# A new head for a fused top-k attention and mixture-of-depths kernel: first rows in order of need, PSUM tiles per head, products that nobody reads, smaller fills

## The chip, the cores and the metric

The kernel runs on one core of a Trainium2 chip. Its time is the device time of one execution in microseconds (us). The core has a matrix engine (TensorE, called PE in the profile), VectorE (DVE), ScalarE (ACT), GpSimd (POOL) and a queue engine that issues transfers (SyncE, SP). ACT can issue transfers as well. Each engine works through its own instructions in the order in which they are written; a wait at the front of a queue holds all that is behind it.

## What is computed

The reference is top-k attention over 8 batches and 8 heads, then a gated two-layer network on 128 chosen rows of each batch:

```python
batch, n_heads, seq, head_dim = (8, 8, 576, 64)          # q, k, v, float32
scores = scale * np.matmul(q, k.transpose(0, 1, 3, 2))
kth = np.partition(scores, -32, axis=-1)[..., -32:-31]    # the 32nd largest of each row
scores = np.where(scores >= kth, scores, -1e9)
attn = softmax(scores);  x = (attn @ v), heads side by side   # (8, 576, 512)
s = x @ w_gate                                            # one score per row
top = the 128 rows of each batch with the largest s
out = x;  out[top] += sigmoid(s[top]) * (relu(x[top] @ w1) @ w2)
```

## The kernel before, in words

**Tiling.** A batch's 576 query rows are four tiles of 128 and one of 64 (`t`). Heads go in pairs. A unit is one row tile with one head pair `g` (in the last, half-filled row tile, with four heads), so a batch has 4 x 4 + 2 = 18 units and the kernel 144 (`units`, `per_batch`). The first four units are row tile 0 of batch 0 with head pairs 0 to 3.

**A unit's way.** PE forms the scores of two heads, 128 x 576 each (`multiply`); ACT copies them from PSUM to the SBUF tile `sc` (`keep`). DVE finds, from maxima of parts of the row, a value `bound` near the 32nd largest (`find_bound`, 14 maxima of 82 or 83 columns, then 10 small steps). ACT compares all scores with it and counts (`sides`), POOL multiplies scores and signs into `y` (`what_is_below`), DVE takes the 8 largest of `y` (`find_kth`), and ACT and POOL mark the scores below the 32nd in `less`, one head each (`mask`). PE transposes scores and adds `less` times a very negative matrix (`weigh`), ACT takes the exponential into `pT`, PE multiplies by `v` (`values`), ACT copies the result to `xs`.

**What sets the order.** The main loop `for n in range(-1, N)` is written out by hand, and the wrapper `InOrder` keeps each engine's instructions in that order. In pass n, DVE does the bound of unit n and the 32nd largest of unit n-2; PE transposes unit n-4, multiplies unit n+1, and does the values of unit n-4; ACT does the exponential of n-4, the mask of n-3, the copy of the scores of n+1, then `sides` of n-1.

**Keys and queries.** Rows of k and q lie in HBM with 64 contiguous floats. They are loaded as rows (`Rows.fetch`, two transfers of 128 KB, one for each head of a pair) and transposed by PE (`Rows.turn`), then copied by ACT into `kT` and `qT` (`Rows.keep`). The rows 512 to 575 of all heads come in a tile of their own, `last` (`turn_last`, `keep_last`). For batch 0 this is done pair by pair ahead of the unit that needs it (`turn_pair`, `turn_all_last`), and the rows stand in the space that the weights `w1` will fill later (`homes`). For the next batches the transposes are cut into 18 parts, which the loop does one or two at a time in spare columns of the scores' PSUM tile (`loads_at`, `first_loads`).

**The head before the change.** SP issues the keys of pair 0, the last rows of k, and then the keys and queries of pairs 1 to 3; ACT issues the queries of pair 0 and the last rows of q. PE runs 48 products of a 128 x 128 bf16 matrix into a tile that nobody reads (`warm_up`); its operand `out_of_reach` is made from the identity, which POOL makes first. Then it transposes all of pair 0 and all last rows, DVE copies the keys, ACT the queries. PSUM has one scores tile of four banks (`ps_sc`), two banks for transposes (`ps_tr`), one for the values (`ps_av`), and one for the rest (`ps_misc`). The first unit's scores are copied half by ACT, half by DVE. POOL fills constants: among them both tiles of `v` (128 x 2,080 floats each) with ones, of which only every 65th is needed.

Of the kernel before, what the change touches and what calls it, by code (L numbers as in the profile page):

```python
# [12 lines left out]
FP32 = mybir.dt.float32  # L13
BF16 = mybir.dt.bfloat16
# [9 lines left out]
SMALLER = 2.0**-20  # L24
# [7 lines left out]
J = 4  # L32
# [16 lines left out]
def kernel(  # L49
# [11 lines left out]
    nc = tc.nc  # L61
    P = nc.NUM_PARTITIONS
    B, H, S, D = q.shape
# [24 lines left out]
        tc.tile_pool(name="dram", bufs=2, space=bass.MemoryType.DRAM)  # L88
    )
    PS = bass.MemoryType.PSUM  # L90
    ps_sc = ctx.enter_context(tc.tile_pool(name="ps_sc", bufs=1, space=PS))
    ps_tr = ctx.enter_context(tc.tile_pool(name="ps_tr", bufs=1, space=PS))
    ps_av = ctx.enter_context(tc.tile_pool(name="ps_av", bufs=1, space=PS))
    ps_misc = ctx.enter_context(tc.tile_pool(name="ps_misc", bufs=1, space=PS))


    ident = const.tile([P, P], FP32, name="ident")
    make_identity(nc, ident)

# [54 lines left out]
    vbufs = []  # L154
    for i in range(2):
        vt = const.tile([P, H, J, DE], FP32, name=f"v{i}")
        nc.gpsimd.memset(vt, 1.0)
        vpair = const.tile([P, NHP, 2, DE], FP32, name=f"vpair{i}")
        nc.gpsimd.memset(vpair, 0.0)
        for hh in range(2):  # L160
            nc.gpsimd.memset(vpair[hh * R : (hh + 1) * R, :, hh, D:DE], 1.0)
        vbufs.append((vt, vpair))

    wg = const.tile([P, HD], FP32, name="wg")
    w1 = const.tile([P, NDC, F], FP32, name="w1")
    w2 = const.tile([P, NFC, HD], FP32, name="w2")

# [46 lines left out]
    class Rows:  # L214
# [1 line left out]

        def __init__(self, kb, qb, kT, qT, issue=None, homes=None):
            self.src, self.kT, self.qT, self.homes = (kb, qb), kT, qT, homes  # L220
            self.last = [
                ldpool.tile([R, H, D], FP32, name=f"last{i}", bufs=1) for i in range(2)
            ]
            self.rows = []
            if issue:
                self.fetch(sp)
                self.fetch(issue)
            for w, dma in enumerate((sp, issue or sp)):
                dma.dma_start(
                    out=self.last[w],  # L230
                    in_=self.src[w][:, JP:S, :].rearrange("h p d -> p h d"),
                )
            while len(self.rows) < (2 * NHP if homes else 2):
                self.fetch()

        def fetch(self, dma=sp):
            i = len(self.rows)
# [20 lines left out]
                    ident[0:R, 0:R],  # L258
                )

        def keep_last(self, w, tr, copy=None):
            copy = copy or act.copy
            tr = tr.rearrange("p b (e r) -> p b e r", e=2)

            def of(a):
                return a.rearrange("p (b e) r -> p b e r", e=2)

            if w == 0:
                copy(out=of(self.kT[:, :, 0:R]), in_=tr)
                copy(out=of(self.kT[:, :, S : S + R]), in_=tr)  # L270
            else:
                act.mul(out=of(self.qT[:, :, JP:S]), in_=tr, mul=SMALLER)
# [12 lines left out]
        def keep(self, i, tr, c0=0, c1=J, copy=None):  # L285
            copy = copy or act.copy
            if i % 2 == 0:
                to = self.kT[:, i // 2, R + c0 * P : R + c1 * P]
            else:
                to = self.qT[:, i // 2, c0 * P : c1 * P]  # L290
            to = to.rearrange("p (c i) -> p c i", i=P)
            if i % 2 == 0:
                copy(out=to, in_=tr)
            else:
                act.mul(out=to, in_=tr, mul=SMALLER)
# [12 lines left out]
                        lambda tr, i=i, c=c: self.keep(i, tr, c, c + 2),  # L308
                    )

    def turn_pair(rows, hp, copy=None):
        tr = ps_tr.tile([P, 2, J, P], FP32, name="ptr")
        for w in range(2):
            rows.turn(2 * hp + w, tr[:, w, :, :])
        for w in range(2):
            rows.keep(2 * hp + w, tr[:, w, :, :], copy=copy)

    def turn_all_last(rows, copy=None):
        tr = ps_misc.tile([P, 2, 2, P], FP32, name="tr", tag="misc")
        for w in range(2):  # L320
            rows.turn_last(w, tr[:, w, :, :])
        for w in range(2):
            rows.keep_last(w, tr[:, w, :, :], copy)

    def load_v(vb, vs):
        vt, vpair = vs
# [25 lines left out]
    def room_for_scores():  # L352
        return ps_sc.tile([P, 2, 2, 512], FP32, name="ps")

    def multiply(t, g, kT, qT, ps):

        n = R if t == J else P  # L360
        for u in range(2):
            for i, heads in enumerate(heads_of(t, g)):
                at = u * HALF + (0 if i else R)
                d = slice(i * D, (i + 1) * D)
                for h, r in heads:
                    pe.matmul(
                        ps[r : r + n, i, u, 0:HALF],
                        qT[d, h // 2, t * P : t * P + n],
                        kT[d, h // 2, at : at + HALF],
                    )  # L370

    def keep(ps, first=False):

        sc = scpool.tile([P, 2, S], FP32, name="sc")
        to = sc.rearrange("p i (u s) -> p i u s", u=2)
        if first:
            for i, copy in enumerate((act.copy, dve.tensor_copy)):
                copy(out=to[:, i, :, :], in_=ps[:, i, :, 0:HALF])
        else:
            act.copy(  # L380
                out=to.rearrange("p i u s -> p (i u) s"),
                in_=ps.rearrange("p i u s -> p (i u) s")[:, :, 0:HALF],
            )
        return sc
# [607 lines left out]


    loads_at = [1, 1, 0, *[1] * 11, 2, 2, 0, 1]
    first_loads = [0, 0, 1, *loads_at[3:]]
    assert sum(loads_at) == sum(first_loads) + 1 == 2 + 4 * NHP
    mix_steps = {}
    for b in range(B - 1):
# [16 lines left out]
    homes = [  # L1015
        homes[:, i, :].rearrange("p (j h d) -> p j h d", j=J, h=2) for i in range(2 * NHP)
    ]
    first_rows = Rows(k[0], q[0], *qkv[0][0:2], issue=act, homes=homes)

    def warm_up():  # L1020
        ps = ps_av.tile([P, 512], FP32, name="av")
        for _ in range(48):
            pe.matmul(ps[:, 0:P], out_of_reach, out_of_reach)

    warm_up()
    turn_pair(first_rows, 0, dve.tensor_copy)
    turn_all_last(first_rows, dve.tensor_copy)
    loading = iter(())
    inverting = normalised = None
    of_batch = {}  # L1030
# [2 lines left out]
    def is_unit(n):  # L1033
        return 0 <= n < N
# [59 lines left out]
    for n in range(-1, N):  # L1094
# [4 lines left out]
                loading, Rows(k[b + 1], q[b + 1], *qkv[b + 1][0:2]).parts()  # L1099
            )  # L1100
        if 0 < n + 1 < NHP:
            turn_pair(first_rows, n + 1)
        if n == 1:
            load_v(v[0], qkv[0][2])
        if n == NHP:
# [21 lines left out]
        flush()  # L1127
        if is_unit(n + 1):
            b, t, g = units[n + 1]
            ps = room_for_scores()  # L1130
            kT, qT = qkv[b][0:2]
            b, i = divmod(n, per_batch)
            loads = list(islice(loading, first_loads[i] if b == 0 else loads_at[i]))
            halves = [ps[:, a, :, HALF : HALF + P] for a in range(2)]
            for load, half in zip(loads, halves):
                load[0](half)
            multiply(t, g, kT, qT, ps)
            for load, half in zip(loads, halves):
                load[1](half)
            scs[n + 1] = keep(ps, n == -1)  # L1140
        if is_unit(n - 4):
            b4, t4, g4 = units[n - 4]
            values(t4, g4, pT, last, av, qkv[b4][2])
# [25 lines left out]
            after_kth.pop(0)()  # L1169


        if is_unit(n - 1):
            what_is_below(n - 1)

        if gating is not None:
# [153 lines left out]
    def general(b, row0):  # L1329
        def of(a):  # L1330
            return a[bass.ds(b, 1)].rearrange("o a s d -> (o a) s d")

        kT, qT, vs = room_for_qkv(0)
        rows = Rows(of(k), of(q), kT, qT)
        turn_all_last(rows)
        for hp in range(NHP):
            turn_pair(rows, hp)
        load_v(of(v), vs)
        x = xpool.tile([P, NT, HD], FP32, name="x")
        pg = gates_of[0]  # L1340
        for t in range(NT):
            xs = xpool.tile([P, H, DE], FP32, name="xs")
            for g in range(groups(t)):
                ps = room_for_scores()
                multiply(t, g, kT, qT, ps)
                p = general_weights(keep(ps))
                tr, av = room_to_turn()
                turn(p, tr)
                pT = ptpool.tile([P, 2, J, P], FP32, name="pT")
                last = ptpool.tile([P, P], FP32, name="last")  # L1350
                nc.scalar.copy(out=pT, in_=tr)
                nc.scalar.copy(out=last, in_=turn_last(p, av))
                values(t, g, pT, last, av, vs)
                keep_values(t, g, av, xs)
            rows = R if t == J else P
            den = stats.tile([P, H], FP32, name="den")
            keep_sums(rows, xs, den[0:rows, :])
            divide(rows, xs, x[0:rows, t, :], den[0:rows, :])
            dot_tile(t, x, pg)
        store(out[bass.ds(b, 1)].rearrange("o s n -> (o s) n"), x)  # L1360
        rank = stats.tile([P, NT], FP32, name="rank")
        for _ in mixture(row0, pg, rank, exact=True):
            flush_all()
        flush_all()
# [40 lines left out]
```

## Time and profile before

| | |
|---|---|
| median of three runs | 826.69 us (826.53 to 827.79) |
| the profiled execution: its own time, its span | 828.44 us, 826.1 us |
| busy share of the span: PE, DVE, ACT, POOL | 94%, 95%, 88%, 87% |
| first maximum on DVE starts | 12.15 us |
| DVE idle from then until 41.44 us | 1.50 + 1.21 + 0.28 us |
| DVE busy from 60 to 80 us, from 300 to 400 us | 20.00 of 20, 99.89 of 100 us |

The span is what the profiler sees between the first and the last instruction; the time of the same execution is 2.3 us longer. "Busy" of an engine leaves out waiting and issuing. The TensorE clock (PEclk) is the share of full speed that the chip granted. Nearly all of the kernel's own instructions stand under one line, L45, the wrapper's, so they are told apart by the tiles that they write and read: `cand<-sc` is a maximum in `find_bound`, `sc<-ps` a copy of scores, `ps<-kT,qT` a product of `multiply`, `ptr<-ident,w` a transpose of first rows.

### The profile page before, as it was taken

How to read it: one execution, taken by the hardware profiler on the slowest of the kernel's cores; microseconds unless marked ns; L12 is line 12 of the kernel's file. 1: busy time of each engine (PE TensorE's matmuls, PEld its weight loads, DVE VectorE, ACT ScalarE, POOL GpSimd, SP SyncE). 2: the span in 40 equal slices, each digit the busy share in tenths (PEclk: the TensorE clock that was granted, in tenths of full speed). 3: DMA queues.
4: the chain of work that ended last, by engine and by line, in shares of the span. 5: the costliest groups of instructions: out<-in, count | busy, mean ns of one | idle time of the engine just before them, and what ended most of it. 6: DMA issues, size and time to landing. Idle time of an engine off the chain costs nothing. (4 is left out here: it accounts for less than half of the span.)

```text
span 826.1 us, 28252 instructions
## 1 busy us (share of the span) xinstructions
PE 777.0 (94%) x10143; PEld 596.5 (72%) x10143; DVE 787.2 (95%) x4651; ACT 730.7 (88%) x1557; POOL 715.4 (87%) x722
## 2 busy tenths in 40 slices
PE   6888888888999999999999999999999999999976
PEld 5566666666887778877787777877787777767744
DVE  7899999999999999999999999999999999999960
ACT  4799999999999999999999999999999999879831
POOL 3799999999899999999899999999999998899831
PEclk9699999999999999999999999999999999999999
DMA  7931111521141221521223221512215102101021
GB/s 170 283 86 40 28 66 28 105 53 27 60 92 36 53 40 59 112 47 34 79 47 86 53 40 60 104 23 54 40 59 112 28 15 66 23 12 18 2 71 30
DMA packets 122133, 50.38 MB, mean 61 GB/s; under 512 B 116417, under 2 KB 116417, under 8 KB 120961
## 3 DMA queue, kind: packets, MB, share of 16 engines
q1 hardware_dynamic: 118672, 43.91, 22.0%
q0 software_dynamic: 1728, 4.20, 2.8%
q8 instruction: 82, 1.34, 0.8%
q14 instruction: 67, 0.54, 0.3%
q10 hardware_dynamic: 1584, 0.39, 0.2%
HBM read 36.93 MB, written 11.55 MB: 59 GB/s over the span
## 5 line engine op out<-in xcount | busy, mean ns | idle before, releaser
L45 POOL TENSOR_TENSOR y<-sc,sides 128x576 f32<-128x576 f32 x288 | 365.1, 1289 | 57.0 <-ACT sides L45 54.3
L45 DVE MAX8 cand<-sc 128x8 f32<-128x82 f32 (+1 forms) x2016 | 314.0, 228 | 2.7 <-ACT sc L45 2.7
L45 POOL TENSOR_SCALAR less<-sc,next 128x576 bf16<-128x576 f32 x135 | 232.5, 1722 | 12.9 <-DVE next L45 10.0
L45 PE MATMUL ptr<-out_of_reach,less 128*128 128x128 bf16 x1136 | 205.3, 220 | 19.5 <-POOL less L45 19.4
L45 ACT ACTIVATE sides<-sc,bound 128x576 bf16<-128x576 f32 x288 | 223.0, 787 | 0.0
L45 PE MATMUL ptr<-ident,sc 128*128 128x128 f32 x1136 | 217.0, 282 | 0.0
L45 DVE MAX8 next<-y 128x8 f32<-128x584 f32 x288 | 204.4, 751 | 1.7 <-POOL y L45 1.6
L45 PEld LDWEIGHTS av<-v,pT 128*64 128x64 f32 x4544 | 144.1, 137 | 66.9 <-ACT last L45 63.2
L45 PE MATMUL ps<-kT,qT 64*128 64x288 f32 (+1 forms) x1280 | 182.0, 431 | 5.2 <-ACT qT L45 5.2
L45 PEld LDWEIGHTS ptr<-ident,sc 128*128 128x128 f32 x1136 | 161.3, 142 | 29.1 <-issue 17.4
L45 ACT ACTIVATE pT<-ptr 128x1024 f32<-128x1024 f32 x142 | 145.3, 1023 | 33.2 <-PE ptr L45 32.2
L45 PE MATMUL av<-v,pT 128*64 128x65 f32 x4544 | 163.7, 224 | 9.3 <-ACT last L45 8.5
L45 ACT COPY sc<-ps 128x1152 f32<-128x1152 f32 (+1 forms) x144 | 162.2, 1126 | 3.5 <-PE ps L45 3.5
L45 PEld LDWEIGHTS <-less 128*128 128x128 bf16 x1296 | 136.1, 106 | 39.2 <-POOL less L45 25.2
L45 PEld LDWEIGHTS ps<-kT,qT 64*128 64x128 f32 (+1 forms) x1280 | 100.2, 178 | 41.5 <-issue 21.2
L45 ACT ACTIVATE less<-sc,next 128x576 bf16<-128x576 f32 x143 | 111.2, 777 | 12.7 <-DVE next L45 10.8
L45 DVE MATCH_REPLACE8 cand<-best,cand 128x21 f32<-128x21 f32 (+1 forms) x576 | 99.0, 180 | 0.0
L45 DVE MAX8 best<-cand 128x8 f32<-128x21 f32 (+1 forms) x576 | 90.5, 190 | 0.0
L45 PE MATMUL h_ps<-xeT,w 128*128 128x128 f32 x464 | 65.8, 286 | 0.0
L45 PEld LDWEIGHTS h_ps<-xeT,w 128*128 128x128 f32 x464 | 55.8, 191 | 9.2 <-issue 5.8
L45 PE MATMUL y_ps<-w,hT 128*128 128x512 f32 x112 | 60.6, 636 | 0.0
L45 ACT ACTIVATION_READ_ACCUMULATOR sides<-sc,bound 128x1 f32 x288 | 59.9, 208 | 0.0
(133 smaller groups left out, 866.4 us busy)
## 6 DMA issues: line engine op xcount, KB each, us to landing
v<-in_v_dram SPq DMA_DIRECT2D x64, 128.0 KB, 4.2
out_dram<-x SPq DMA_DIRECT2D x8, 1024.0 KB, 3.9
rows<-in_k_dram SPq DMA_DIRECT2D x56, 128.0 KB, 2.9
rows<-in_q_dram SPq DMA_DIRECT2D x56, 128.0 KB, 3.1
w<-in_moe_w_dram SPq DMA_DIRECT2D x2, 2048.0 KB
gate_row<-row_dram SPq DMA_DIRECT2D x7, 288.0 KB, 4.4
w<-in_k_dram SPq DMA_DIRECT2D x8, 128.0 KB, 3.2
last<-in_k_dram SPq DMA_DIRECT2D x8, 128.0 KB, 4.0
```

What stands on the lines that cost most here:

```text
L45: return lambda *a, **kw: self._tc.keep_in_program_order(fn(*a, **kw))
```

## The change

The change rewrites what happens until the fifth unit:

- **First rows by need, two queues.** `fetch_first` issues the keys of head 0 on SP and of head 1 on ACT, then on SP the one column of pair 0's queries that row tile 0 needs (64 KB), on ACT the last keys of heads 0 and 1 (32 KB), then the other query columns and last keys on both. The last rows of q come at the end of SP's list.
- **Only what the next unit needs is transposed.** `FirstPairs.first` turns the keys of pair 0, one query column and the last keys of two heads: six transposes instead of sixteen. `turn` does the same for a later pair. The other query columns follow in two blocks, at n = 0 and n = 3, the last rows of q at n = 3.
- **PSUM tiles per head.** The first four units use two tiles of two banks, `one` and `two`, one for each head; ACT copies each head's scores on its own (128 x 576), also the half of unit 0 that DVE copied. The pool is closed after unit 3, and the four banks become `ps_sc`.
- **Unread products in TensorE's gaps.** `stay_busy` runs 30 products at the start, from a part of `wg` that DVE sets to zero, and 10, 10, 20, 30 and 20 after the multiplications of units 0 to 4.
- **`sides` of unit n-1 before the scores of unit n+1** on ACT, in the passes n = 1 and 2.
- **Short fills.** POOL sets only the 32 columns of ones in each `v` tile.
- The 18 parts of batch 1 start one pass later (`first_loads`).

```diff
+    wg = const.tile([P, HD], FP32, name="wg")
+    nothing = wg[:, 0 : P // 2].bitcast(BF16)
+    nc.vector.memset(nothing, 0.0)
...
-        nc.gpsimd.memset(vt, 1.0)
+        nc.gpsimd.memset(vt[:, :, :, D:DE], 1.0)
...
+        def fetch_first(self):
+            k_rows, q_rows = self.homes[0:2]
...
+            sp.dma_start(out=k_rows[:, :, 0, :], in_=of(0, 0, 0, J))
+            act.dma_start(out=k_rows[:, :, 1, :], in_=of(0, 1, 0, J))
+            sp.dma_start(
+                out=q_rows[:, 0, :, :],
+                in_=self.src[1][0:2, 0:JP, :].rearrange("h (p j) d -> p j h d", j=J)[
+                    :, 0, :, :
+                ],
+            )
+            self.fetch_last(0, act, 0, 2)
+            sp.dma_start(out=q_rows[:, 1:J, 0, :], in_=of(1, 0, 1, J))
+            act.dma_start(out=q_rows[:, 1:J, 1, :], in_=of(1, 1, 1, J))
+            self.fetch_last(0, act, 2, H)
+            while len(self.rows) < 2 * NHP:
+                self.fetch()
+            self.fetch_last(1)
...
+        def first(self):
...
+            rows.turn(0, k01, 0, half)
+            rows.turn(0, k23, half, J)
+            rows.turn(1, q0.unsqueeze(1), 0, 1)
+            self.turn_last_keys(range(1), last)
+            rows.keep(0, k01, 0, half, copy=dve.tensor_copy)
+            rows.keep(0, k23, half, J)
+            dve.tensor_scalar_mul(rows.qT[:, 0, 0:P], q0, SMALLER)
+            self.keep_last_keys(range(1), last)
+
+        def turn(self, hp):
+            rows = self.rows
+            keys = bank(ps_av, "av").rearrange("p (c i) -> p c i", i=P)
+            some = bank(ps_misc, "some", tag="misc")
+            rest = range(1, NHP) if hp == 1 else range(0)
+            last = some[:, P : P + len(rest) * R]
+            rows.turn(2 * hp, keys)
+            self.turn_last_keys(rest, last)
+            rows.turn(2 * hp + 1, some[:, 0:P].unsqueeze(1), 0, 1)
+            rows.keep(2 * hp, keys)
+            if rest:
+                self.keep_last_keys(rest, last)
+            rows.keep(2 * hp + 1, some[:, 0:P].unsqueeze(1), 0, 1)
...
-    first_loads = [0, 0, 1, *loads_at[3:]]
+    first_loads = [0, 0, 0, *[1] * 11, 2, 2, 1, 1]
...
-    def warm_up():
-        ps = ps_av.tile([P, 512], FP32, name="av")
-        for _ in range(48):
-            pe.matmul(ps[:, 0:P], out_of_reach, out_of_reach)
-
-    warm_up()
-    turn_pair(first_rows, 0, dve.tensor_copy)
-    turn_all_last(first_rows, dve.tensor_copy)
+    def stay_busy(times, what=out_of_reach):
+        ps = bank(ps_av, "av")
+        for _ in range(times):
+            pe.matmul(ps[:, 0:P], what, what)
+
+    stay_busy(30, nothing)
+    first_pairs.first()
...
         if 0 < n + 1 < NHP:
-            turn_pair(first_rows, n + 1)
+            first_pairs.turn(n + 1)
+        if n == 0:
+            for hp in range(2):
+                first_pairs.turn_queries(hp)
+            for hp in range(2):
+                first_pairs.keep_queries(hp)
+        if n == NHP - 1:
+            for hp in range(2, NHP):
+                first_pairs.turn_queries(hp)
+            for hp in range(2, NHP):
+                first_pairs.keep_queries(hp)
+            first_pairs.last_queries()
+            first_steps.close()
+            ps_sc = ctx.enter_context(tc.tile_pool(name="ps_sc", bufs=1, space=PS))
...
+            if n + 1 < NHP:
+                ps = room_for_first_scores()
+                multiply(t, g, kT, qT, ps)
+                if is_unit(n - 1):
+                    what_is_below(n - 1)
+                stay_busy((10, 10, 20, 30)[n + 1])
+            else:
...
+                if n == NHP - 1:
+                    stay_busy(20)
+            scs[n + 1] = keep(ps)
...
-        if is_unit(n - 1):
+        if is_unit(n - 1) and n + 1 >= NHP:
             what_is_below(n - 1)
```

## The prediction

> **What bounds the kernel now.** I read the page's busy rows first, then the stretches, then the timeline of each engine in the first 45 us.
>
> ```profile
> PE   6888888888999999999999999999999999999976
> DVE  7899999999999999999999999999999999999960
> PEclk9699999999999999999999999999999999999999
> ```
>
> Each digit is a fortieth of the span, 20.7 us. DVE is full except in the first two slices and at the end, so it bounds the kernel: what DVE gains in the first two slices reaches the end, if nobody else becomes the bound. In the second slice the TensorE clock stands at 0.6. The stretches say the same with numbers (columns: busy us of PE, weight loads, DVE, ACT, POOL; clock; DMA):
>
> ```profile
> 20.00:30.00 10.00, 6.68 (x29) 4.28 (x29) 8.47 (x54) 6.97 (x15) 6.22 (x7) 0.55 0.81 209
> 40.00:50.00 10.00, 9.51 (x144) 7.20 (x138) 9.91 (x61) 10.00 (x21) 9.34 (x10) 1.00 0.67 147
> 300.00:400.00 100.00, 98.12 (x1316) 76.01 (x1313) 99.89 (x599) 95.40 (x205) 92.28 (x91) 1.00 0.28 60
> ```
>
> From 300 to 400 us DVE rests 0.11 us, and ACT, the next non-PE engine, has 4.6% to spare. Now DVE's timeline (start, length, what; in brackets the idle time before and who ended it):
>
> ```profile
> 2.63 4.09 DVE L143 CAST steps<-steps_i 128x16 f32<-128x16 int32 x1
> 8.14 0.69 DVE L45 COPY kT<-ptr 128x512 f32<-128x512 f32 x1 [1.41 <-PE ptr L45]
> 11.48 0.76 DVE L45 COPY sc<-ps 128x576 f32<-128x576 f32 x1 [1.94 <-ACT sc L45]
> 12.15 2.13 DVE L45 MAX8 cand<-sc 128x8 f32<-128x82 f32 x14
> 25.39 2.14 DVE L45 MAX8 cand<-sc 128x8 f32<-128x82 f32 x14 [1.50 <-ACT sc L45]
> 36.30 2.14 DVE L45 MAX8 cand<-sc 128x8 f32<-128x82 f32 x14 [1.21 <-ACT sc L45]
> 40.09 1.44 DVE L45 MAX8 next<-y 128x8 f32<-128x584 f32 x2 [0.28 <-POOL y L45]
> ```
>
> DVE starts its real work at 12.15 and then loses 1.50 + 1.21 + 0.28 = 2.99 us until 41.44; after that it hardly waits. Two things to win: an earlier start, and those 2.99 us. The timelines of PE, ACT and POOL name the causes:
>
> ```profile
> 1.69 5.30 PE L45 MATMUL av<-out_of_reach 128*128 128x128 bf16 x48 [1.69 <-DVE out_of_reach L126]
> 6.79 1.31 PE L45 MATMUL ptr<-ident,w 128*128 128x128 f32 x8
> 16.40 1.24 PE L45 MATMUL ps<-kT,qT 64*128 64x288 f32 x8 [1.18 <-ACT qT L45]
> 21.36 2.29 PE L45 MATMUL ps<-kT,qT 64*128 64x288 f32 x8 [2.03 <-ACT qT L45]
> 23.69 0.65 ACT L45 COPY kT<-ps 128x256 f32<-128x256 f32 x2 [2.39 <-PE ps L45]
> 2.57 1.84 POOL L157 MEMSET v<- 128x2080 f32 x1
> 4.82 1.84 POOL L157 MEMSET v<- 128x2080 f32 x1
> ```
>
> PE's warm-up ends only at 6.7. The same eight products take 1.24 us at 16.40 and 2.29 at 21.36: the clock fell to half at 21.0 and came back at 34.65 (records of the trace), and that is where the scores of units 3 and 5 are late. In POOL's and DVE's lines a cast of 16 columns takes 4.09 us; it ends at 6.72, just after POOL's second large fill (6.66), while a cast of 128 columns took 0.35.
>
> [...] warm-up products come every 0.107 us, the clock rose at 7.34, and 7.34, 20.99 and 34.65 are 13.65 us apart[...] here, from 7.34 to 20.99, PE was busy some 64% of the time by the profile (9 of 14 us), much of it transposes, and lost its clock. [...] 238 GB/s for both queues together from 3 to 6 us.
>
> **The change, step by step.** All against the profiled execution (span 826.1; its own time 828.44, 1.75 above the median of 826.69; a saving carries over to the median unchanged).
>
> *Start.* The zeros come from DVE's first instruction (0.8) and no longer from POOL's identity, so PE starts at about 1.0 instead of 1.69. 30 products x 0.107 = 3.2: PE is free at 4.2. Loads: the first transfers issued on either queue landed at 3.5 and 3.9 before, so both keys of pair 0 are there at 3.9. Ahead of the query column stand 128 KB on its queue and as much on the other: about 384 KB at 230 GB/s after a start at 2.1 is 3.8, plus the 0.6 by which landings trailed, 4.4 to 4.6; needed at 5.1. Hidden. Price if late: 1:1.
>
> *First unit.* Five transposes at half clock (0.213 apart, as at 6.79) and one small one (0.125): 4.2 to 5.4, result 5.7. DVE copies the first keys (0.43) and scales the query column (128 columns from PSUM: no row; between the 0.23 of a 128-column SBUF operation and 0.42 of a 256-column copy, I take 0.27); ACT's last copy of keys (about 0.29, as its 128-column ones) ends at 6.0. DVE is free for it only because of the short fills: with the old ones its cast would hold it until 6.7, 1.7 us late. Two products more on ACT's issue queue end at 3.4 and its table load (1.28) at 4.7, ahead of its first copy at 5.2. Product 6.1 to 8.35 at half clock, 7.8 if the clock rises at 7.3 as before. ACT's first half of the scores (0.64, the row at 10.80) gives DVE its start at 8.5 to 9.0. I take 8.8: 3.35 earlier than 12.15.
>
> *Second unit.* DVE is free at 8.8 + 3.41 = 12.2. At full clock: ten unread products (0.5), eight transposes (0.9) until the query column, ACT busy until 11.3 with the second half (0.55), keys (0.49), last keys (0.4), column (0.2) and the two query blocks (0.8); product 10.3 to 11.6; scores 12.3. At half clock until 10.7 it is 13.0 to 13.4. Wait 0.1 to 0.9; I take 0.4. The keys of pair 1 land at about 7.2 (7.4 and 7.8 before, with 128 KB less ahead now), needed at 8.4.
>
> *Units 2 to 5.* ACT now does `sides` (1.53 from start to start) ahead of the scores' copies: scores of unit 2 are ready near 15.5, DVE wants them at 16.0; of unit 3 near 19.0, wanted at 20.8, after `find_kth` (1.36). Unit 4: PE has 30 unread products (1.6), six transposes, eight small ones and the product behind unit 3's; its scores come near 23.8, wanted at 25.5. Unit 5 hangs on the transposes of unit 0, 1.7 us at full clock (3.9 at half): ready near 29.2, wanted near 30.3. So no wait while the clock holds. Before, PE stood 1.18 + 1.18 + 2.03 us in these gaps; now 90 products (90 x 0.053 = 4.8 us) stand in them, and from about 17 to 24 PE has no gap at all[...]. That is why I expect no second fall of the clock. DVE saves 2.99 - 0.4 = 2.6.
>
> *Cost.* ACT: per-head copies 4 x 2 x 0.55 against 0.55 + 3 x 1.0, +0.85; split queries about +0.8; unit 0's other half and keys from DVE about +1.2. All of it stands in gaps of at least 1 us that ACT has now (1.34, 1.34, 2.39, 0.64, 0.85, 1.08). The later start of batch 1's parts ends in the same pass, 17; SP's order behind the head is unchanged, one issue longer (0.63), 5 us ahead of need. The `w1` load waits for PE's last transposes of first rows, now at about 21; SP reached it at 24. Nothing on the path.
>
> Sum: 3.35 + 2.6 = 5.95, less 0.1 for ACT's fuller pipe: about **5.9 us**, a span of 820.2 and a median of **820.8**.
>
> **Rivals.** *The clock rises late* [...]: the rise comes at 11 to 18 instead of 7. Each of units 1 to 3 then needs about 5 us of PE and ACT in series (1.07 + 1.07 + 0.7 + 2.3) against DVE's 3.4 to 4.8, so DVE waits 1.6 to 2.7 at unit 1 and up to 1.6 at unit 2. Gain 2.5 to 5: 822 to 824. For it: the rise at 7.34 came after 5.6 us of products without a gap, and now a gap follows the sixth transpose. Against: at half clock PE is packed from 6 on[...]. *The clock falls again at about 20* although fed: unit 5 then waits about 1.5 and unit 6 another 1, as before: gain 3 to 4, 823. *The start is bound by transfers*: landing of head 1's keys like the 6.34 of the second SP transfer before: gain 3.5 to 4.5. *DVE's gain is taken back* by a transfer or ACT in the next 50 us: 0.5 to 2 us gained; against: rows and `v` land several us before use. *Slower*: half clock all through the head[...]. Waits of 2.4, 1.6, 1.3 and then about 1.5 for each unit eat 6 us once the half clock lasts to about 27; at 35 it costs 3 us: 830. *Better*: the clock rises at 5, gain 7 or more.
>
> **How the numbers follow.** Main case (gain 5.0 to 6.9) 0.60, late rise, second fall or late transfers (2.5 to 5) 0.24, taken back (0.5 to 2) 0.05, slower 0.04, better (over 6.9) 0.07. Main case's own range 819.8 to 821.7. For 8 in 10: 819.3 to 823.6. Within 0.2% (1.65 us, about what a measurement here can tell from no change) 0.04, faster 0.92, slower 0.04.
>
> **What would show it.** DVE's first `cand<-sc` at 8.5 to 9.2, its cast of `steps` under 1.5 us; `sc<-one` releasing the second unit with under 1 us of idle time, and no wait over 0.5 us on DVE from the third unit to 35 us; clock 1.00 from 11 us on, and products of 1.24 us. DVE's maxima of unit 6 (41.44 before) at about 35.5. Wrong if the clock is half in 20 to 30 us again, if the first product waits on a transfer, or if DVE rests more than 0.2 us per 100 us later on.

## The result and the profile after

The changed kernel takes 822.13 us (median of 6 runs, 821.54 to 823.20), the kernel before in the same runs 826.61 (6 runs, 824.87 to 827.79). The ratio is 0.9946, with a 95% interval of 0.9935 to 0.9957: 4.5 us faster, where 5.9 were forecast. The profiled execution of after took 821.91 us (span 819.7).

The busy rows of the page of after (a digit is a fortieth of the span):

```profile
PE   8998888888999999999999999999999999999976
DVE  7999999999999999999999999999999999999960
PEclk9999999999999999999999999999999999999999
```

and its stretches (busy us of PE, weight loads, DVE, ACT, POOL; clock; DMA):

```profile
20.00:30.00 10.00, 9.41 (x128) 7.74 (x125) 10.00 (x63) 8.81 (x20) 7.16 (x7) 1.00 0.86 215
40.00:50.00 10.00, 9.46 (x135) 7.19 (x134) 9.96 (x64) 9.97 (x23) 9.40 (x9) 1.00 0.81 160
300.00:400.00 100.00, 98.48 (x1299) 76.69 (x1297) 99.89 (x606) 95.01 (x204) 92.10 (x90) 1.00 0.26 59
```

The 0.6 in the clock's second slice is gone, and from 20 to 30 us DVE is busy all 10 us instead of 8.47. DVE's timeline of after (start, length, what; in brackets the idle time before and who ended it):

```profile
2.63 1.14 DVE L149 CAST steps<-steps_i 128x16 f32<-128x16 int32 x1
5.17 0.42 DVE L45 COPY kT<-av 128x256 f32<-128x256 f32 x1 [1.40 <-PE av L45]
7.93 2.13 DVE L45 MAX8 cand<-sc 128x8 f32<-128x82 f32 x14 [2.06 <-ACT sc L45]
12.00 2.13 DVE L45 MAX8 cand<-sc 128x8 f32<-128x82 f32 x14 [0.56 <-ACT sc L45]
15.54 2.13 DVE L45 MAX8 cand<-sc 128x8 f32<-128x82 f32 x14
34.50 2.12 DVE L45 MAX8 cand<-sc 128x8 f32<-128x82 f32 x14
```

The first maximum comes at 7.93 instead of 12.15, the second unit waits 0.56, and from there to unit 6 nothing waits; unit 6's maxima start at 34.50 instead of 41.44, 6.94 earlier. PE's timeline of after shows where that comes from, and something else:

```profile
0.99 3.38 PE L45 MATMUL av<-wg 128*128 128x128 bf16 x30 [0.99 <-DVE row L1505]
4.48 0.66 PE L45 MATMUL av<-ident,w 128*128 128x128 f32 x2
7.27 0.73 PE L45 MATMUL av<-out_of_reach 128*128 128x128 bf16 x10
8.06 0.66 PE L45 MATMUL av<-ident,w 128*128 128x128 f32 x4
17.56 0.51 PE L45 MATMUL one<-kT,qT 64*128 64x288 f32 x1 [0.74 <-ACT qT L45]
18.73 1.85 PE L45 MATMUL av<-out_of_reach 128*128 128x128 bf16 x30
20.41 0.82 PE L45 MATMUL ptr<-ident,w 128*128 128x128 f32 x6
22.84 1.29 PE L45 MATMUL av<-out_of_reach 128*128 128x128 bf16 x20
```

The unread products stand right before transposes (7.27 before 8.06, 18.73 before 20.41), while PE's idle time (0.74) comes after them, in front of the next product, where it waits for ACT's copies of just those transposes. So they don't fill the gaps: they lengthen the chain of product, transposes, copies and next product. What that costs is the main finding below.

### The profile page after: what moved, and what is told of

Read it like the earlier page. It is cut to its first block, busy times and chain, and to the rows that moved or that the text cites. A ratio compares the mean times of both kernels' runs of the same rounds, so it can differ in the third digit from the quotient of the medians.

```text
span 819.7 us, 28408 instructions
## 1 busy us (share of the span) xinstructions
PE 776.4 (95%) x10215; PEld 597.1 (73%) x10215; DVE 782.5 (95%) x4650; ACT 732.2 (89%) x1567; POOL 713.3 (87%) x722
## 5 line engine op out<-in xcount | busy, mean ns | idle before, releaser
L45 PE MATMUL ps<-kT,qT 64*128 64x288 f32 (+1 forms) x1248 | 173.9, 425 | 0.0
L45 ACT COPY sc<-ps 128x1152 f32<-128x1152 f32 x140 | 158.3, 1131 | 0.0
L45 ACT ACTIVATE less<-sc,next 128x576 bf16<-128x576 f32 x143 | 111.2, 778 | 13.2 <-DVE next L45 11.6
L45 PEld LDWEIGHTS ps<-kT,qT 64*128 64x128 f32 (+1 forms) x1248 | 95.8, 175 | 34.5 <-issue 20.8
```

The source lines that it names most:

```text
L45: return lambda *a, **kw: self._tc.keep_in_program_order(fn(*a, **kw))
```

## The experiments

The theory after the result was the prediction's: an earlier start and a held clock, both at no cost. The rivals: the products cost time; the clock needs none of them; the gain over the profiled execution isn't the gain over a usual one. The runs come in sets; the median of the kernel before was 826.61 us in the first set and 825.93, 825.67 and 826.18 in the three later ones, so differences of medians between sets are uncertain by about half a microsecond.

**The kernel before once more, and with the products alone.** The first is a copy of the kernel before, 22 runs. The second adds only the 90 products, after the multiplications of units 0 to 4:

```diff
             multiply(t, g, kT, qT, ps)
+            if n + 1 <= NHP:
+                idle = ps_av.tile([P, 512], FP32, name="av")
+                for _ in range((10, 10, 20, 30, 20)[n + 1]):
+                    pe.matmul(idle[:, 0:P], out_of_reach, out_of_reach)
```

> The kernel before, unchanged, to see how its own executions spread. Theory A (the loss of the clock is a matter of chance): its executions differ in the granted clock, from about 0.990 (a second half-clock stretch of 13.65 us, as in the first profile) to 0.998 (none), and the times go with it: about 828 with the long stretch, 825 to 826 without; the median lies between, so the 6.4 us that the two profiles differ by overstate the typical gain. Theory B (the clock falls each time): clock 0.990 in every execution, times within 0.5 us of each other, and the missing 2 us lie elsewhere.

> The kernel before with nothing but the unread products in TensorE's gaps (10, 10, 20, 30, 20 after the multiplications of units 0 to 4). Theory A: the clock stays at full speed after its rise, DVE's 1.50 and 1.21 us waits shrink to under 0.6 together, unit 6 starts on DVE near 39 instead of 41.4, and the kernel is 1.5 to 2.5 us faster than before by the median. Rival (the order of ACT's copies, not the clock, made the waits): no change within 0.7 us.

The copy took 825.80 (823.89 to 829.49), ratio 0.9998 [0.9989, 1.0007]. With the products: 825.40 (825.04 to 826.79, 13 runs), ratio 0.9999 [0.9991, 1.0007]. One stretch of each, before and then with the products:

```profile
20.00:35.00 15.00, 11.03 (x56) 7.06 (x58) 13.47 (x84) 10.04 (x22) 11.19 (x11) 0.54 0.89 278
```

```profile
20.00:35.00 15.00, 12.05 (x157) 9.68 (x157) 14.40 (x91) 12.55 (x27) 11.57 (x12) 1.00 0.95 284
```

The products do hold the clock (1.00 instead of 0.54; times of its rise and fall, here and below, are from the records of the trace), and against the profiled execution of before DVE gains 2.5 us by unit 6 (38.94 instead of 41.44). Of these, 0.8 us stand at the first maximum already (11.35 instead of 12.15), where the clock rose at 5.68 instead of 7.34, ahead of any of the 90 products. But the median hardly moves, and the 1.5 to 2.5 us that were expected don't come. Two things are behind that. First, the profiled execution of before is not a usual one. All 85 executions of that kernel in three sets of runs, sorted by their mean granted clock:

| mean clock | executions | median us | range |
|---|---|---|---|
| 0.990 to 0.991 (the profiled one: 0.990, with 13.65 us at half clock) | 25 | 827.20 | 826.69 to 829.49 |
| 0.992 to 0.993 | 53 | 825.71 | 824.11 to 826.93 |
| 0.994 to 0.995 | 7 | 824.72 | 823.83 to 825.30 |

So the executions that lost more of the clock are slower, and the profiled ones (828.44, and 829.04 of the copy) are of the slowest group. Second, with the products the clock is 0.998 to 1.000 and the time still 825.4, above the 824.72 of executions that lost some clock. This points to a cost of the products themselves, which the next run shows.

**After without the 90 gap products.** The 30 at the start stay:

```diff
-                stay_busy((10, 10, 20, 30)[n + 1])
...
-                if n == NHP - 1:
-                    stay_busy(20)
```

> The changed kernel without the 90 products in the gaps; the 30 at the start stay. Theory A: the clock, which rose at 5.1 in the changed kernel, falls about 13.65 us later, at 18 to 21, DVE waits 1.5 to 2.5 us in all around units 4 to 6, and the time is 1.5 to 2.5 us above the changed kernel's (824 instead of 822). Rival (with units that come faster PE's own work holds the clock, the products are idle freight): clock 0.998, same as the changed kernel within 0.5 us.

817.40 (817.27 to 819.31, 4 runs), ratio 0.9907 [0.9893, 0.9921]. That is 4.7 us *faster* than the changed kernel (about 4 when each is taken against the kernel before in its own set), and the clock stands at 0.998 to 0.999 without them. The rival had the clock right; neither forecast had the time. PE's timeline of this kernel, then ACT's:

```profile
7.37 0.66 PE L45 MATMUL av<-ident,w 128*128 128x128 f32 x4
12.82 0.51 PE L45 MATMUL one<-kT,qT 64*128 64x288 f32 x1 [1.24 <-ACT qT L45]
```

```profile
18.40 0.95 ACT L45 ACTIVATE qT<-ptr 128x384 f32<-128x384 f32 x2
```

The transposes follow the product at once. In after, ACT waits for PE before the same copy, and does it 2.87 us later (its timeline):

```profile
21.27 0.87 ACT L45 ACTIVATE qT<-ptr 128x384 f32<-128x384 f32 x2 [1.19 <-PE ptr L45]
```

DVE sees little of it in the head: unit 8's bound ends at 46.98 instead of 47.52. But ACT and POOL stay late, and this comes out at the product of `x` and `wg`, an operation of DVE that reads two SBUF tiles. DVE's timeline of after, then POOL's:

```profile
50.22 1.76 DVE L45 CUSTOM_DVE_ANT_0 prod<-x,wg 128x512 f32<-128x512 f32 x1 [0.26 <-POOL x L45]
91.30 1.75 DVE L45 CUSTOM_DVE_ANT_0 prod<-x,wg 128x512 f32<-128x512 f32 x1
```

```profile
49.13 1.05 POOL L45 TENSOR_TENSOR x<-xs,rden 128x512 f32<-128x512 f32 x1
50.13 2.99 POOL L45 TENSOR_TENSOR y<-sc,sides 128x576 f32<-128x576 f32 x2
91.23 2.98 POOL L45 TENSOR_TENSOR y<-sc,sides 128x576 f32<-128x576 f32 x2
```

and the same two without the gap products, DVE and POOL:

```profile
49.26 1.12 DVE L45 CUSTOM_DVE_ANT_0 prod<-x,wg 128x512 f32<-128x512 f32 x1
89.56 0.67 DVE L45 CUSTOM_DVE_ANT_0 prod<-x,wg 128x512 f32<-128x512 f32 x1
```

```profile
46.31 1.04 POOL L45 TENSOR_TENSOR x<-xs,rden 128x512 f32<-128x512 f32 x1
47.31 2.52 POOL L45 TENSOR_TENSOR y<-sc,sides 128x576 f32<-128x576 f32 x2
88.34 3.02 POOL L45 TENSOR_TENSOR y<-sc,sides 128x576 f32<-128x576 f32 x2
```

In after DVE reaches its product just when POOL has finished `x` and begun a `y`: it waits 0.26 and then takes 1.76 us, and POOL's two `y` take 2.99 instead of 2.52. Without the gap products POOL does `x` 2.8 us earlier and DVE its product only 1.0 us earlier, so POOL has nearly finished the second `y` by then. At the third product the difference is plainest. In after DVE comes 0.07 us after POOL has begun the first of two `y` and takes 1.75 us. Without the gap products it comes 1.22 us into such a pair, about where the first `y` ends, and takes 0.67; there it is POOL's pair that takes longer, 3.02 us. So the same product takes 0.67 to 1.76 us by where it meets POOL's `y`; what holds it up there the traces don't show.

**A lag without products.** If it is the lag of ACT behind DVE that costs, any delay of ACT must do the same. Four copies that nobody reads, on ACT, in the kernel without gap products:

```diff
             scs[n + 1] = keep(ps)
+            if n == NHP - 1:
+                for _ in range(4):
+                    act.copy(out=wg, in_=scs[n + 1][:, 0, 0:HD])
```

> The kernel without the 90 gap products, with four ACT copies of 512 columns that nobody reads, after the copy of unit 4's scores (about 0.5 us each, 2.0 to 2.2 us together; the time without them is 817.4). Theory of the lag: the gap products cost time because they put ACT and POOL about 2.3 us further behind DVE, ACT has no slack to make it up, and DVE's operations later meet POOL's. Then any delay of ACT of that size does the same: ACT's copy of unit 4's xs moves from 45.45 to about 47.6 us, DVE's first product of x and wg waits about 0.26 us and takes about 1.75 us again, and the time is 820.5 to 822.3. Rival, that the cost lies in the products themselves, on TensorE: 817.3 to 818.0, the copies disappear in ACT's gaps or are made up.

821.73 (820.44 to 823.07, 5 runs), ratio 0.9947 [0.9934, 0.9961]. ACT's and DVE's timelines:

```profile
22.00 2.58 ACT L45 COPY wg<-sc 128x512 f32<-128x512 f32 x4
```

```profile
51.89 1.75 DVE L45 CUSTOM_DVE_ANT_0 prod<-x,wg 128x512 f32<-128x512 f32 x1 [0.26 <-POOL x L45]
```

The 4.3 us are back, with the same wait and the same long product. In the profiled execution (823.07) the clock also fell, for 6.83 us from 26.0 on, and 2.1 us of its loss against the kernel without gap products lie before the end of unit 8's bound; but the two executions with a mean clock of 1.000 took 821.63 and 821.73, so the lag suffices (their times show that; no trace of them was kept).

**Some of the products.** After with the 10, 10 and 20 only:

```diff
-                stay_busy((10, 10, 20, 30)[n + 1])
+                if n + 1 < NHP - 1:
+                    stay_busy((10, 10, 20)[n + 1])
...
-                if n == NHP - 1:
-                    stay_busy(20)
```

> The changed kernel with only the first 40 gap products (10, 10 and 20, after the products of units 0 to 2); the 30 and 20 after units 3 and 4 are out. Theory of the lag: by the scores' copies of unit 3 the first 40 have put ACT 1.5 us back (18.9 against 17.4 us) of some 2.7 in all at unit 4 (23.5 against 20.8), so more than half of the 4.7 us should remain: 819.5 to 821. Rival, that only the groups of 30 and 20, which stand ahead of the transposes of unit 0, cost: 817.4 to 818.2. Rival, that the lag acts like a switch: near 822.

818.75 (818.12 to 820.64), ratio 0.9918 [0.9904, 0.9933]: neither nothing nor all, between the ranges of the forecast and of the first rival.

**`sides` back behind the scores.** In the kernel without gap products, the order of ACT in passes 1 and 2 as before:

```diff
-                if is_unit(n - 1):
-                    what_is_below(n - 1)
...
-        if is_unit(n - 1) and n + 1 >= NHP:
+        if is_unit(n - 1):
             what_is_below(n - 1)
```

> The kernel without the 90 gap products, with the sides of units 0 and 1 back behind the copies of the scores of units 2 and 3 on ACT. My working said that DVE is wanted by neither order: scores of units 2 and 3 come 1.5 us earlier, which nobody needs, y of units 0 and 1 1.3 us later, needed 2 us later still: 817.2 to 817.8. Rival, that the change needs this order, because POOL's y and with it all masks come later and the lag behind DVE grows by 1.3 us: 819 to 820.5.

819.94 (819.68 to 820.92, 6 runs), ratio 0.9926 [0.9912, 0.9941]: 2.5 us lost, as the rival said. ACT's timeline:

```profile
13.69 0.64 ACT L45 COPY sc<-one 128x576 f32<-128x576 f32 x1 [1.32 <-PE two L45]
18.37 0.64 ACT L45 COPY sc<-one 128x576 f32<-128x576 f32 x1 [1.33 <-PE two L45]
```

The change does `sides` in the 1.3 us in which ACT stands idle here, waiting for PE; now `sides` comes afterwards and holds up the copies of the next keys, and with them PE. PE's timeline:

```profile
17.09 0.51 PE L45 MATMUL one<-kT,qT 64*128 64x288 f32 x1 [2.74 <-ACT qT L45]
18.28 1.54 PE L45 MATMUL ptr<-ident,w 128*128 128x128 f32 x6
```

Before the product of unit 3 it waits 2.74 us instead of 1.30, and then the clock falls as well, from 18.2 to 21.6 us, so that the six transposes take 1.54 us instead of 0.87. Unit 3's product starts 1.04 us later than in the kernel without gap products, ACT's copy of unit 4's scores 2.40 us later (23.15 instead of 20.75). So the order and the clock that it loses both have a part in the lag; how the 2.5 us divide between them isn't shown. The masks and all that follows come later.

Put beside each other, from the profiled execution of each kernel (lead: how long before DVE ends the bound of unit 8 ACT starts the exponential of unit 4; then DVE's time from the end of unit 8's bound to that of unit 18's; the first and third product of `x` and `wg`):

| kernel | lead, us | units 8 to 18, us | products, us |
|---|---|---|---|
| before | 2.19 | 52.69 | 1.75, 1.75 |
| before with 90 products | 2.21 | 52.65 | 1.75, 1.75 |
| after | 2.23 | 52.69 | 1.76, 1.75 |
| without gap products, ACT delayed | 2.16 | 52.74 | 1.75, 1.75 |
| without gap products, `sides` behind | 2.21 | 52.66 | 1.75, 1.75 |
| after with 40 gap products | 3.56 | 51.31 | 0.85, 1.75 |
| without gap products | 4.52 | 50.39 | 1.12, 0.67 |

With a lead of 2.2 us ten units cost 2.3 us more than with 4.5: just the difference of the leads. The other kernels below fit: with the large fills 2.28 and 52.59, without any unread product, with the old order of loads and in the last two 4.50 to 4.53 and 50.36 to 50.44. ACT's exponentials of units 4 and 14, in after and then without gap products, show why:

```profile
45.28 1.00 ACT L45 ACTIVATE pT<-ptr 128x1024 f32<-128x1024 f32 x1
96.92 1.02 ACT L45 ACTIVATE pT<-ptr 128x1024 f32<-128x1024 f32 x1 [1.00 <-PE ptr L45]
```

```profile
42.46 1.00 ACT L45 ACTIVATE pT<-ptr 128x1024 f32<-128x1024 f32 x1
94.07 1.02 ACT L45 ACTIVATE pT<-ptr 128x1024 f32<-128x1024 f32 x1 [1.04 <-PE ptr L45]
```

ACT takes the same 51.6 us for these ten units in both, and in every kernel here (51.57 to 51.66); and everywhere DVE ends the bound of unit 18 3.3 us (3.28 to 3.30) after the second of these exponentials starts. So when DVE gets through unit 18 follows from when ACT gets to unit 4, and not from DVE's own time at unit 8: with the old order of loads DVE is 2.2 us later than after at unit 8 (49.71 and 47.52), but 0.1 us earlier at unit 18 (100.11 and 100.21), since ACT starts unit 4's exponential at 45.21 and 45.28. Why ACT's ten units take the same time in all of them isn't shown.

After unit 18 the kernels with a lead of 2.2 differ among themselves: to the bound of the last unit, after needs 1.3 us more than the kernel without gap products (671.39 against 670.13), the one with `sides` behind 0.5 less (669.67). I can name two waits in after's part of that, 0.55 us at 420.7 for another operation of DVE and 1.85 instead of 1.31 us for a transfer at 714 (0.81 with the large fills, 0.86 with `sides` behind), but not why they come; that stays open.

**The products before, fewer.** The kernel before with 10, 10 and 20:

```diff
+            if n + 1 < 3:
+                idle = ps_av.tile([P, 512], FP32, name="av")
+                for _ in range((10, 10, 20)[n + 1]):
+                    pe.matmul(idle[:, 0:P], out_of_reach, out_of_reach)
```

> The kernel before with unread products only after units 0 to 2 (10, 10 and 20); the 30 and 20 that the earlier run with all 90 had in addition are out. That run took as long as the kernel before (825.4 against 825.9) although its clock stayed at 0.999, and in the kernel before the executions with a mean clock of 0.995 take 823.8 to 824.8, those with 0.990 take 826.8 to 829.5. Theory that two effects cancel there (the held clock gains, the lag of ACT and POOL behind DVE costs as much): with fewer products the lag is smaller, and where the clock holds (0.998 or more) the time is 822.5 to 824.5. Rival, that the half clock costs a usual execution nothing: 825.0 to 826.2 at any clock. If the clock falls all the same (0.996 or less) the run tells nothing on this and will be near 825.

826.83 (825.63 to 828.24, 14 runs), ratio 1.0008 [0.9999, 1.0017]. The clock falls all the same (mean 0.992 to 0.996; in the profiled execution from 24.2 to 34.4 us), so this doesn't show what a held clock is worth with a smaller lag. At a mean clock of 0.992 its five executions have a median of 827.68, the three of the kernel before in the same set 826.50: that fits a price of the products but is too few to show one. Nor can it be the lag, if there is one: the lead with 90 products is 2.21 us, without them 2.19. That in the run with 90 products gain and price cancel is thus argued, not shown.

**The start: no unread product at all.**

```diff
-    stay_busy(30, nothing)
```

(on the kernel without gap products)

> The changed kernel without any unread product, the 30 at the start out as well. Theory that the start needs them: the clock rises only [...] at 8 to 11 us instead of 5.4, transposes and product of units 0 and 1 run at half clock, the first maximum comes about 1 us later (9.0 instead of 8.03) and unit 1 waits some 1 to 2 us: 818.5 to 820.5. Rival, that TensorE's own work from 4.2 us on raises the clock nearly as soon: 817.0 to 817.8, with the transposes starting 0.3 us earlier because nothing has to drain from their tile.

819.19 (819.03 to 819.81), ratio 0.9919 [0.9905, 0.9933]. DVE's timeline:

```profile
8.90 2.13 DVE L45 MAX8 cand<-sc 128x8 f32<-128x82 f32 x14 [3.11 <-ACT sc L45]
13.51 0.68 DVE L45 MAX8 cand<-sc 128x8 f32<-128x82 f32 x4 [1.11 <-ACT sc L45]
```

The first maximum is 0.87 us later and the second unit waits 1.11: the clock rises only at 11.6, and the 30 products at the start are worth 1.8 us.

**The order of the first loads**, as before, in the kernel without gap products:

```diff
-            act.dma_start(out=k_rows[:, :, 1, :], in_=of(0, 1, 0, J))
...
+            sp.dma_start(out=k_rows[:, :, 1, :], in_=of(0, 1, 0, J))
+            act.dma_start(out=q_rows[:, :, 0, :], in_=of(1, 0, 0, J))
+            act.dma_start(out=q_rows[:, :, 1, :], in_=of(1, 1, 0, J))
+            self.fetch_last(0)
+            self.fetch_last(1, act)
```

> The kernel without the 90 gap products, with the first loads in the order of before: both heads' keys on SP, both heads' whole queries on ACT, then all last keys on SP and all last queries on ACT. Theory that the order by need is worth time: the last keys and the query blocks have 500 to 650 KB ahead of them and land at 5.6 to 6.5 instead of about 5.0, the first product starts 0.7 to 1.3 us later, and as DVE is the bound from there, the time is 818.2 to 818.9 against 817.4. Rival, that the transfers are hidden behind the 30 products and the transposes: 817.2 to 817.8.

822.15 (820.33 to 822.61, 6 runs), ratio 0.9950 [0.9935, 0.9964]: 4.7 us lost, far more than I expected. PE's timeline:

```profile
6.11 0.41 PE L45 MATMUL av<-ident,w 128*128 128x128 f32 x2 [1.80 <-DMA w<-in_k_dram]
7.08 0.27 PE L45 MATMUL two<-ident,last 64*128 64x64 f32 x1 [0.23 <-DMA last<-in_k_dram]
```

The keys of head 1, second on SP's queue behind those of head 0 and beside two whole queries on ACT's, hold the first transposes until 6.11 instead of 4.48. In the stall PE loses the clock that the 30 products had won (up at 4.1, down at 7.5, up again at 10.9), so that unit 1's bound ends 2.7 us later. The profiled execution (820.33) is the fastest of the six; where the others lose up to another 2.3 us their times don't tell (two of the five have a mean clock of 0.994, the other three 0.999).

**The large fills of `v` back**, in after:

```diff
-        nc.gpsimd.memset(vt[:, :, :, D:DE], 1.0)
+        nc.gpsimd.memset(vt, 1.0)
```

> The changed kernel with the large fills of v put back. If GpSimd's fills hold DVE's cast of steps, the cast ends at about 6.7 instead of 3.8, DVE's copy of the first keys starts at 6.7 instead of 5.2, the first maximum at 9.3 instead of 7.9, and the kernel is 1.2 to 1.5 us slower than the changed one. Rival (the cast's length is its own affair, or other waits cover it): the first maximum moves less than 0.3 us and the time stays.

821.08 (820.66 to 823.12, 5 runs), ratio 0.9956 [0.9943, 0.9969]. DVE's timeline:

```profile
2.63 4.09 DVE L149 CAST steps<-steps_i 128x16 f32<-128x16 int32 x1
5.18 1.55 DVE L45 COPY kT<-av 128x256 f32<-128x256 f32 x1
```

The cast takes 4.09 us again instead of 1.14, and the copy of the first keys ends at 6.73, just after the second large fill (6.65). The first maximum comes 0.90 us later (8.83), and unit 6 ends 0.83 later; yet at the end nothing of it can be measured, where 1.2 to 1.5 us were expected. In the profiled execution the later part has less of what after loses beyond unit 18 (669.66 against 671.39).

**Towards a better kernel.** Without gap products, with the 30 at the start in the tile of `ptr` (PE need not drain them before it writes `av`), and half of unit 0's scores copied by DVE again; then also three more unread products between the first transposes and the first product:

```diff
-    stay_busy(30, nothing)
+    unread = ps_tr.tile([P, 2, J, P], FP32, name="ptr")
+    for _ in range(30):
+        pe.matmul(unread[:, 0, 0, :], nothing, nothing)
...
-                act.copy(out=to[:, i, :, :], in_=ps[i][:, :, 0:HALF])
+                copy = dve.tensor_copy if first and i == 1 else act.copy
+                copy(out=to[:, i, :, :], in_=ps[i][:, :, 0:HALF])
```

```diff
             self.turn_last_keys(range(1), last)
+            meanwhile(3)
```

> The kernel without the 90 gap products, in which DVE copies the second head's scores of unit 0, as it did before the change (0.65 us, in a stretch in which DVE waits; ACT is 0.53 us freer), and the 30 products at the start write to the tile of ptr instead of av, so that the first transposes need not wait for them to drain (0.28 us). Theory: first maximum at 7.75 instead of 8.03, ACT's lead over DVE grows by about 0.5 us, time 816.6 to 817.2 against 817.4. Rival, that the phase in which DVE meets POOL gives it back: 817.4 to 818.5.

> As the kernel of the last call that had the start's unread products in the tile of ptr and DVE copying half of unit 0's scores (817.58), with three more unread products between the first transposes and the first product, where TensorE stood 0.18 us. In the profiled execution of that kernel the clock rose only at 10.25 us, in those of the other kernels with 30 products at 4.3 to 5.7. Theory: [...] with TensorE busy without a gap from 1.0 to 8 us [...] all executions are near the lowest seen, 816.7 to 817.3, with a spread under 1 us. Rival, that the gap had nothing to do with it: 817.3 to 818 and executions up to 819.

The first took 817.58 (816.94 to 818.66, 4 runs), ratio 0.9896 [0.9881, 0.9911]; the second 817.09 (816.92 to 818.23, 5 runs), ratio 0.9893 [0.9877, 0.9909]. PE's timeline of the first, then of the second:

```profile
4.17 0.63 PE L45 MATMUL av<-ident,w 128*128 128x128 f32 x2
5.92 0.81 PE L45 MATMUL one<-kT,qT 64*128 64x288 f32 x1 [0.18 <-DVE qT L45]
```

```profile
5.29 0.34 PE L45 MATMUL ptr<-wg 128*128 128x128 bf16 x3
5.62 0.48 PE L45 MATMUL one<-kT,qT 64*128 64x288 f32 x1
```

The transposes do start 0.31 us earlier (4.17), but ACT's lead does not grow (4.53 in both, 4.52 without gap products). In the first kernel's profiled execution the first product still ran at half clock (0.81 instead of 0.48; rise at 10.25), although PE had been busy from 0.99 to 5.7. In the profiled executions of the eight other kernels with 30 products the clock rose at 4.1 to 5.5 us. Why it rose so late in this one stays open. Whether the three products settle it isn't shown: four of five executions lie within 0.31 us of each other at the low end, one is at 818.23. Both kernels beat the kernel before and the changed one; between them and the kernel without gap products (817.40) the intervals overlap.

## Why the prediction was right, and where it was not

**The time.** 822.1 lies in the range, 1.3 us above the number: the profiled executions differ by 6.53 us (828.44 and 821.91), the medians by 4.5. That the number came so close is partly luck. The working followed DVE, but the time at unit 18 goes with ACT. Both came earlier by nearly the same amount (ACT's exponential of unit 4 by 7.01 us, DVE's bound of unit 8 by 6.96), so DVE's sum served for ACT too; the kernel without gap products, in which ACT's lead is larger, took 817.4, outside the range.

**The sum against the profiled execution: confirmed and a little small.** The steps *Start* and *First unit* gave 3.35 us together and were 4.22: PE was free at 4.4 (4.2 forecast), keys landed at 3.8 (3.9), and the query column at about 5, still unseen; but the clock rose at 5.12, before the first product, where I had half clock until 7.3. That was the condition of the rival *Better*, though not its gain of 7 or more. *Second unit*: 0.56 us of wait for 0.4. *Units 2 to 5*: no wait, as forecast. DVE's cast under 1.5 us (1.14) and the clock of 1.00 from 11 us on were there; unit 6 came at 34.5, forecast 35.5. *DVE's gain is taken back* happened in a small form, 0.4 of 6.94 us by the end.

**What failed: "a saving carries over to the median unchanged".** The 2.99 us of waits in *Units 2 to 5* came from a clock that was halved for 13.65 us. By the mean clock, 25 of 85 executions of before lose that much; the usual one loses less. The profiled execution stood 1.8 us above its median, and I put that down to a constant, when the page showed a cause that varies.

**What failed: "Nothing on the path" in *Cost*, and "now 90 products (90 x 0.053 = 4.8 us) stand in them" in *Units 2 to 5*.** The products stand ahead of the transposes, on the chain from PE to ACT and back, not in PE's idle time. They cost 4.7 us by the medians of the runs with and without them. Of the 4.4 us between the two profiled executions 0.54 have come at unit 8 and 2.3 more from unit 8 to 18; the other 1.6 come later, and that they are the products' isn't shown. I had counted ACT's room in the head and found DVE not waiting. But ACT doesn't make up what it lost: its exponential of unit 4 is 2.82 us later than without the products, that of unit 14 still 2.85, and DVE, which meets POOL at a worse moment at its first and third product of `x` and `wg`, falls back by as much. Against the kernel before nothing is lost by this, as its lead is the same 2.2 us; what the working missed is a gain that the products gave away.

**What failed: the reason for the clock.** "That is why I expect no second fall" was right in the fall and wrong in the why: without gap products the clock stands at 0.999 as well. In the head of that kernel PE waits up to 1.30 us at a time (0.38, 1.24 and 1.30 us), and the clock holds. Two falls went with longer waits: in the kernel before the clock fell at 21.0 us, in the midst of a wait of 2.03 us, the longest that PE had had by then, and with `sides` behind at 18.2 us, 1.1 us after a wait of 2.74. At what point a wait costs the clock isn't shown, nor why the executions of the kernel before differ in clock: only its two profiled ones have a trace. The 30 at the start are needed (1.8 us).

**Parts that I gave no price of their own.** The order of `sides` (2.5 us, the clock that it holds included) and the first loads (4.7 us, likewise) carry more of the gain than I saw: in my working the one served only DVE's next wait, and the other only the start.

## What to carry to other kernels

A filler costs nothing only if it stands where the engine would otherwise wait: put it behind the instructions that others wait for, not ahead of them (the runs show the price of the place ahead; the 90 were not tried behind), and take it out alone once to see its price. An engine that seems not to be the bound can keep a delay of the start until the bound engine has it too, as ACT did here from 45 to 97 us; look at its lead over the bound engine after the start, not only at the bound engine's waits. Before a saving is counted against a profiled execution, ask whether what it saves occurs in every execution.

## What was not expected of the hardware

- The same DVE product of 128 x 512 from two SBUF tiles takes 0.67 to 1.76 us, by where it falls among POOL's operations. A lead of ACT that differed by 2.3 us made 2.3 us in ten units, while ACT took the same 51.6 us for them.
- The mean granted clock of the executions of one kernel lay between 0.990 and 0.995, and their time followed it: 827.2, 825.7 and 824.7 us in the median.
- Thirty unread products from 1.0 to 4.4 us raised the clock at 4.1 to 5.5 us in eight profiled executions, and at 10.25 in one.
- In the kernel before the clock fell in the midst of a wait of PE of 2.03 us and then stood at half for 13.65 us; without gap products it held through waits of 1.24 and 1.30 us.
